# Low parts of the sequence-DFT pieces: GpSimd's subtraction replaced by a negated copy on ScalarE and an accumulating transfer from DRAM

## The chip, the cores and the metric

The kernel runs on one core of one Trainium2 chip. The metric is the device time of one execution in microseconds (us). Beside the timed runs there is one execution recorded by the hardware profiler; its span runs from the first to the last instruction of the program. The engines are named as the profile names them: PE (matrix products; PEld is its weight load), DVE (VectorE), ACT (ScalarE), POOL (GpSimd), and SP, which only issues transfers.

## What is computed

The input is one sequence of 2048 tokens with 640 features, x. Two branches are mixed with a gate per token:

```
g   = sigmoid((x * gate_w).sum(-1))
a   = x @ hid_re.T            b = x @ hid_im.T
A   = seq_re @ a - seq_im @ b                  # real part of a 2-D DFT
s1, s2 = scores of 32 heads against two sets of 16 keys
B   = sum over heads and the best 2 of 256 experts of  gate * gelu(x.u_e) * v_e
out = g * A + (1 - g) * B
```

`seq_re` and `seq_im` are 2048 x 2048, `hid_re` and `hid_im` 640 x 640, all float32. The change concerns `seq_re` and `seq_im` alone.

## The kernel before

**Three products for one.** PE multiplies in fp32r, a float32 with a shorter mantissa. To keep the precision, each float32 matrix is split in two: a high part h, which is the matrix rounded to fp32r, and a low part l = f - h. A product is then three fp32r products, high x high, high x low, low x high (`mm3`, L127 to L129). The helper `split` writes h on ScalarE (L122) and l by a subtraction on the engine that it is given (L123), so all splits in the profile have these two lines, and are told apart by their tiles.

**The sequence product.** The kernel does the sequence part of the DFT first, then the hidden part. The two sequence matrices are cut in 128 pieces of 128 x 512 (256 KB each): two matrices (`w`), four column blocks of 512 (`c`), 16 row tiles (`s`). In one step, `seq_piece(n)`, PE multiplies the five 128-wide slices of the split x tile `X[s]` with piece n and adds to five PSUM banks: 15 matmuls of 128x512. After 16 steps ScalarE copies the five banks to the tile `ST` (L217), DVE multiplies with the gate row (L191), and the result goes to the DRAM scratch `pd` (L198).

**How a piece comes in.** Step n issues the load of piece n+5 on SP's queue into one of five float32 buffers `wf` (L158), then splits piece n+3 into one of the four slots of the tile `WS`: each slot has a high and a low half. So at step n the slot of piece n-1 is written again, which has to wait until PE is through with piece n-1; and what is written is read by PE three steps later. In a step, the first matmul takes h (L127), the second takes l (L128).

**The start.** Piece 0 is split on ScalarE and VectorE. Pieces 1 and 2 are split before the loop, on ScalarE and GpSimd. Between their subtractions and that of piece 3 stand, on GpSimd's queue, the constants of other stages: `kp` (L286), `io` (L288), `identf` (L290), `ident` (L292) and an iota table (L294).

**What shares the steps.** Through the first 16 steps the tiles of x are loaded (`xr`, L235), split, and summed with the gate weights (L255). From step 4 to about step 30, the weights of the score branch `wq` (32 loads of 640 KB, five buffers, `load_wq`, L305) are folded with the keys on PE (L314), transposed and split; a load of `wq` is issued when the matmuls of the load five before it are done. Steps 31 to 70 carry the scores of a token tile (`score_half`) and its top-2 search on DVE. From step 71 on come the split of the hidden matrices into `DD` (`split_dd`, one subtraction on GpSimd in each of ten steps), and then `experts`: one-hot matrices built on DVE (L567 to L569), multiplied on PE (L595), moved out by ScalarE (L576). The last steps prepare sums of the hidden matrices (`ts`), and after step 127 follows the hidden product in 70 steps (L848), which takes its operands from `pd` with the same `split`, the low parts on GpSimd or VectorE, in a ring of the tiles `WP` and `WS`.

**What sets the order.** Each engine runs its own instructions in the order in which the program was written (the table `then` and the credit of `Pump` decide where a background piece is put in); semaphores hold an instruction until its inputs are there. An instruction that waits holds all that stand behind it on its engine. Transfers are issued on SP's queue and on ScalarE's; GpSimd issues none.

Of the kernel before, what the change touches and what calls it, by code (L numbers as in the profile page):

```python
# [8 lines left out]
F32 = mybir.dt.float32  # L9
F32R = mybir.dt.float32r  # L10
F16 = mybir.dt.float16
AF = mybir.ActivationFunctionType
OP = mybir.AluOpType
# [77 lines left out]
def gated_mix_kernel(ctx: ExitStack, tc: tile.TileContext, xT, xn, dreT, dimT, wsre, wsim, wq, kT, uT, vv, gw, out):  # L91
    nc = tc.nc
# [27 lines left out]
    def split(f, h, l, eng):  # L120

        nc.scalar.activation(h, f, AF.Copy)  # L122
        eng.tensor_sub(l, f, h.bitcast(F32))  # L123
# [27 lines left out]
    pieces = [(w, c, s) for w in range(2) for c in range(NC) for s in range(NT)]  # L151
    pf, psp, X, xr = {}, {}, {}, {}
# [7 lines left out]
    WS = big.tile([P, 4, 2, TC], F32R, name="WS", tag="WS")  # L160

    def split_piece(n):
        if n < NPC:
            psp[n] = WS[:, n % 4, 0], WS[:, n % 4, 1]
            split(pf.pop(n), *psp[n], nc.gpsimd)


    then = {}
# [31 lines left out]
    def seq_piece(n):  # L200
        w, c, s = pieces[n]
        if s == 0:
            banks[:] = [bank(d) for d in range(KD)]
        load_piece(n + 5)
        split_piece(n + 3)
        h, l = psp.pop(n)
        if n == 0:
            for a, (x, c) in enumerate(((0, h), (0, l), (1, h))):
                for d in range(KD):
                    nc.tensor.matmul(banks[d], X[0][:, x, d * P:(d + 1) * P], c, start=a == 0, stop=False)  # L210
            return
        for d in range(KD):
            ds = slice(d * P, (d + 1) * P)
            mm3(banks[d], X[s][:, 0, ds], X[s][:, 1, ds], h, l, s == 0, s == NT - 1)
            if s == NT - 1:
                staged[n // NT, d] = f = stage()
                nc.scalar.activation(f, banks[d], AF.Copy)  # L217
            run_bg(0.68)

    for q in range(2 * NC):  # L220
        n = NT * (q + 1)
# [58 lines left out]
    for n in (1, 2):  # L280
        split_x(n)
        split_piece(n)
# [84 lines left out]
    n = bursts[-1]  # L367
# [170 lines left out]
    for p in range(NP):  # L538
        n = N0 + 5 * p
# [467 lines left out]
```

## Time and profile before

| | us |
|---|---|
| median of 3 runs | 777.33 |
| lowest and highest | 776.52, 777.54 |
| the profiled execution | 775.9 |
| its span | 774.1 |

| engine | busy us | share of the span | instructions |
|---|---|---|---|
| PE | 768.1 | 99% | 4628 |
| DVE | 502.2 | 65% | 594 |
| ACT | 283.3 | 37% | 461 |
| POOL | 342.9 | 44% | 233 |

The granted clock of PE was full through the span. The profiled execution took 1.8 us more than its span: what lies around the instructions. It lies 1.4 us under the median of the timed runs. In the profile, a row of the timeline is: start, length, engine, line, operation, tiles (out<-in), shape, and in brackets the idle time before it with what ended it. A row of a window table is: the window, its length, per engine the busy time and the number of instructions, the granted clock, the mean busy share of the core's 16 DMA engines, and what they moved in GB/s. A DMA row gives the number of issues, the size of each, and the time from issue to landing.

### The profile page before, as it was taken

To read this page: it belongs to the slowest core of one execution; us is meant where nothing else is said; L and a number is where in the kernel's file an instruction comes from. 1 tells how busy PE (TensorE), PEld (TensorE's weight loads), DVE (VectorE), ACT (ScalarE), POOL (GpSimd) and SP (SyncE) were. 2 spreads that over 40 slices of the span, in tenths; PEclk is the share of its full clock that TensorE was granted. 3 is DMA by queue.
4 is the path that set the end of the run, shared out by engine and by line. 5 is a ranking of instruction groups with operands and counts; after the bars stand their busy time and mean duration, and the time that the engine had idled before them with its cause. 6 is when DMAs were issued, how large, how long until landed. Compare 5 with 4: busy or idle time off the path is not lost.

```text
span 774.1 us, 11926 instructions
## 1 busy us (share of the span) xinstructions
PE 768.1 (99%) x4628; PEld 622.2 (80%) x4628; DVE 502.2 (65%) x594; ACT 283.3 (37%) x461; POOL 342.9 (44%) x233
## 2 busy tenths in 40 slices
PE   9999999999999999999999999999999999999997
PEld 6777677888888888888888888777788888888886
DVE  6641121276888698689978593687677488628561
ACT  5344323322214432353343453322243453424350
POOL 5523224415144242424332885343346583659270
PEclk9999999999999999999999999999999999999999
DMA  9976985603021530224324454453564694766321
GB/s 349 357 269 192 307 327 191 209 0 116 15 102 35 168 130 2 90 61 136 113 72 151 141 163 112 97 165 92 151 194 160 201 313 162 256 190 203 123 82 68
DMA packets 86792, 121.20 MB, mean 157 GB/s; under 512 B 33104, under 2 KB 40144, under 8 KB 86736
## 3 DMA queue, kind: packets, MB, share of 16 engines
q1 hardware_dynamic: 57344, 100.90, 40.1%
q10 hardware_dynamic: 29392, 19.54, 8.1%
q8 instruction: 36, 0.59, 0.3%
q14 instruction: 20, 0.16, 0.1%
HBM read 98.91 MB, written 19.93 MB: 154 GB/s over the span
## 4 chain that ended last, share of the span: by engine, by line
PE 97%; POOL 1%; DMA 1%; ACT 0%; SPq 0%; issue 0%; ACTq 0%; DVE 0%; DVEq 0%; POOLq 0%
PE b L127 31%; PE b L128 31%; PE b L129 31%; PE b L314 3%; PE b L595 1%; DMA wf<-in_wsre 1%; PE b L326 1%; POOL WS L123 0%; POOL kp L286 0%; ACT L384 0%; SPq L235 0%; SPq L158 0%; POOL identf L290 0%; ACT WS L122 0%; ACT ST L217 0%
## 5 line engine op out<-in xcount | busy, mean ns | idle before, releaser
L123 POOL TENSOR_TENSOR WS<-wf,WS 128x512 fp32r<-128x512 f32 x127 | 190.6, 1506 | 278.0 <-ACT WS L122 256.6
L127 PE MATMUL b<-WS,X 128*128 128x512 f32 x635 | 251.2, 396 | 0.1
L128 PE MATMUL b<-WS,X 128*128 128x512 f32 x635 | 247.9, 390 | 0.2 <-POOL WS L123 0.2
L129 PE MATMUL b<-WS,X 128*128 128x512 f32 x635 | 247.4, 390 | 0.0
L127 PEld LDWEIGHTS b<-WS,X 128*128 128x128 f32 x635 | 119.2, 188 | 33.3 <-issue 7.8
L129 PEld LDWEIGHTS b<-WS,X 128*128 128x128 f32 x635 | 119.2, 188 | 25.2
L128 PEld LDWEIGHTS b<-WS,X 128*128 128x128 f32 x635 | 119.3, 188 | 24.6 <-POOL WS L123 1.1
L122 ACT ACTIVATE WS<-wf 128x512 fp32r<-128x512 f32 x128 | 80.8, 632 | 111.9 <-PE b L129 59.4
L431 DVE TENSOR_REDUCE mm<-sc 128x64 f32<-128x1024 f32 x32 | 39.0, 1219 | 46.2 <-ACT sc L417 45.6
L123 POOL TENSOR_TENSOR xl<-xf,xh 128x640 fp32r<-128x640 f32 x16 | 33.1, 2089 | 70.3 <-ACT xh L122 62.9
L127 PE MATMUL b<-WU,xh 128*128 128x512 f32 x160 | 62.2, 389 | 0.0
L128 PE MATMUL b<-WU,xh 128*128 128x512 f32 x160 | 62.2, 389 | 0.0
L129 PE MATMUL b<-WU,xl 128*128 128x512 f32 x160 | 62.2, 389 | 0.0
L123 POOL TENSOR_TENSOR WS<-ra,WS 128x512 fp32r<-128x512 f32 x32 | 46.2, 1469 | 27.4 <-ACT WS L122 27.4
L417 ACT ACTIVATE sc<-b 128x512 f32<-128x512 f32 x32 | 20.8, 650 | 101.9 <-PE b L129 100.8
L567 DVE TENSOR_TENSOR hot<-rows,wtab 128x1024 f16<-128x1024 f16 x32 | 29.9, 935 | 35.7 <-PE b L595 35.7
L191 DVE SCALAR_TENSOR_TENSOR ST<-ST,grow 128x512 f32<-128x512 f32 x40 | 34.2, 912 | 22.4 <-DMA grow<-gdr 15.5
L433 DVE TENSOR_TENSOR eq<-sc,mm 128x1024 f16<-128x1024 f32 x32 | 45.3, 1416 | 1.1
L741 DVE TENSOR_TENSOR ra<-ra 128x512 f32<-128x512 f32 x40 | 40.7, 1066 | 6.1 <-POOL WS L123 6.1
L329 DVE TENSOR_TENSOR WU<-b,WU 128x512 fp32r<-128x512 f32 (+1 forms) x16 | 7.8, 491 | 56.6 <-ACT WU L328 56.6
L123 POOL TENSOR_TENSOR WP<-ra,WP 128x512 fp32r<-128x512 f32 x18 | 30.4, 1696 | 27.2 <-ACT WP L122 21.5
L497 ACT ACTIVATE rows<-rt 128x384 f16<-128x384 f16 x16 | 31.0, 1968 | 25.3 <-DMA rt<-gs 25.3
(141 smaller groups left out, 1190.6 us busy)
## 6 DMA issues: line engine op xcount, KB each, us to landing
wq<-in_wq SPq DMA_DIRECT2D x32, 640.0 KB, 6.2
ra<-pd SPq DMA_DIRECT2D x70, 256.0 KB, 4.1
wf<-in_wsre SPq DMA_DIRECT2D x64, 256.0 KB, 4.9
wf<-in_wsim SPq DMA_DIRECT2D x64, 256.0 KB, 2.8
pd<-ST ACTq DMA_DIRECT2D x40, 256.0 KB, 3.1
xr<-in_xn SPq DMA_DIRECT2D x16, 320.0 KB, 6.1
xf<-in_xT SPq DMA_DIRECT2D x16, 320.0 KB, 3.2
out_y<-ST ACTq DMA_DIRECT2D x7, 512.0 KB, 3.6
```

The costliest lines, as they stand in the source:

```text
L122: nc.scalar.activation(h, f, AF.Copy)
L123: eng.tensor_sub(l, f, h.bitcast(F32))
L127: nc.tensor.matmul(o, wh, ah, start=first, stop=False, skip_group_check=more)
L128: nc.tensor.matmul(o, wh, al, start=False, stop=False, skip_group_check=more)
L129: nc.tensor.matmul(o, wl, ah, start=False, stop=last, skip_group_check=more)
L191: nc.vector.scalar_tensor_tensor(f, f, -1.0 if w else 1.0, g, op0=OP.mult, op1=OP.mult)
L314: nc.tensor.matmul(ps[32 * j:32 * j + 32, :HALF], kp[:, 8 * G // H, r, :], w[:, j], start=(r == 0), stop=(r == 1))
L431: nc.vector.tensor_reduce(m, sc, op=OP.max, axis=AX.X)
L433: nc.vector.tensor_tensor(eq, sc, m[:, :, None].to_broadcast([P, HH, E]), op=OP.is_equal)
L497: nc.scalar.activation(ROWS[i // 8][:, :, :, i % 8], t, AF.Copy)
L567: nc.vector.tensor_tensor(pt, row(0), wt, op=OP.is_equal)
L741: nc.vector.tensor_add(raw[b, o, k], raw[b, o, k], raw[b, what, k])
```

## The change

Pieces 0, 1 and 2 are split as before. For the other 125 pieces, ScalarE writes h as before, then a second ScalarE instruction reads h and writes -h into the low half of the slot; then GpSimd's queue issues a transfer that reads the same piece from DRAM once more and adds it to what the low half holds, so that it becomes f - h. The subtraction on GpSimd goes. The piece is thus read from DRAM twice, and the low half is ready when the transfer has landed.

```
     def split_piece(n):
         if n < NPC:
-            psp[n] = WS[:, n % 4, 0], WS[:, n % 4, 1]
-            split(pf.pop(n), *psp[n], nc.gpsimd)
+            psp[n] = h, l = WS[:, n % 4, 0], WS[:, n % 4, 1]
+            f = pf.pop(n)
+            if n < 3:
+                split(f, h, l, nc.gpsimd)
+                return
+            w, c, s = pieces[n]
+            nc.scalar.activation(h, f, AF.Copy)
+            nc.scalar.activation(l, h.bitcast(F32), AF.Copy, scale=-1.0)
+            nc.gpsimd.dma_start(l, (wsre, wsim)[w][c, s], accum_op=OP.add)
```

The lines behind it move down by seven; in the changed kernel L170 writes h, L171 writes -h and L172 is the transfer.

How the instructions stand is shown at three places. The first is GpSimd's queue at the start, from the subtractions of pieces 1 and 2 to the last constant and what comes behind it. Before:

```order
L123 TENSOR_TENSOR WS<-wf,WS 128x512 x2
L286 COPY kp<-kt 128x2x16 x2
L288 IOTA io 128x128
L290 TENSOR_SCALAR identf<-io 128x128
L292 CAST ident<-identf 128x128
L294 IOTA wtab_147 128x64
L123 TENSOR_TENSOR WS<-wf,WS 128x512 x28
```

And in the changed kernel:

```order
L123 TENSOR_TENSOR WS<-wf,WS 128x512 x2
L293 COPY kp<-kt 128x2x16 x2
L295 IOTA io 128x128
L297 TENSOR_SCALAR identf<-io 128x128
L299 CAST ident<-identf 128x128
L301 IOTA wtab_147 128x64
L172 DMA WS<-in_wsre 128x512 x28
```

The transfers stand where the subtractions stood: that of piece 3 is still behind the constants.

The second place is ScalarE's queue at the end of the first 16 steps, around the sigmoid of the gate (`gt`) and the copies of the five banks to `ST`. Before:

```order
L384 ACT_TABLE_LOAD
L384 ACTIVATE gt<-zc 128x16
L385 DMA gdr<-gt 128x16x1
L122 ACTIVATE WS<-wf 128x512
L217 ACTIVATE ST<-b_149 128x512
```

And in the changed kernel:

```order
L391 ACT_TABLE_LOAD
L391 ACTIVATE gt<-zc 128x16
L392 DMA gdr<-gt 128x16x1
L170 ACTIVATE WS<-wf 128x512
L171 ACTIVATE WS<-WS 128x512
L224 ACTIVATE ST<-b_149 128x512
```

The write of -h has come between the write of h and the first copy of a bank; so it does at every piece, ahead of whatever ScalarE had next.

The third place is GpSimd's queue in the steps that split the hidden matrices. Before:

```order
L123 TENSOR_TENSOR DD<-draw,DD 128x640
L123 TENSOR_TENSOR WS<-wf,WS 128x512
L123 TENSOR_TENSOR DD<-draw,DD 128x640
L123 TENSOR_TENSOR WS<-wf,WS 128x512
L123 TENSOR_TENSOR DD<-draw,DD 128x640
```

And in the changed kernel:

```order
L123 TENSOR_TENSOR DD<-draw,DD 128x640
L172 DMA WS<-in_wsim 128x512
L123 TENSOR_TENSOR DD<-draw,DD 128x640
L172 DMA WS<-in_wsim 128x512
L123 TENSOR_TENSOR DD<-draw,DD 128x640
```

A transfer stands between two subtractions of `DD` and is issued in turn with them.

## The prediction

> **What bounds the kernel now.** I read the page first: busy shares, chain, and the two groups that the change touches.
>
> ```profile
> PE 768.1 (99%) x4628; PEld 622.2 (80%) x4628; DVE 502.2 (65%) x594; ACT 283.3 (37%) x461; POOL 342.9 (44%) x233
> ...
> PE 97%; POOL 1%; DMA 1%; ACT 0%; SPq 0%; issue 0%; ACTq 0%; DVE 0%; DVEq 0%; POOLq 0%
> ...
> L123 POOL TENSOR_TENSOR WS<-wf,WS 128x512 fp32r<-128x512 f32 x127 | 190.6, 1506 | 278.0 <-ACT WS L122 256.6
> ...
> L122 ACT ACTIVATE WS<-wf 128x512 fp32r<-128x512 f32 x128 | 80.8, 632 | 111.9 <-PE b L129 59.4
> ```
>
> PE is busy 99% of the span and carries 97% of the chain. The subtractions cost 190.6 us on GpSimd, but GpSimd is 44% busy. Next, the waits of PE: who could give it time back?
>
> ```profile
> PE b L274 <- DVE warm L271: 1.2, 1, 1.2
> PE b L210 <- ACT WS L122: 0.5, 1, 0.5
> PE b L128 <- POOL WS L123: 0.2, 1, 0.2
> ```
>
> That is the whole list. PE waits 0.2 us for GpSimd in all, at piece 3. So a lighter GpSimd gives PE at most 0.2 us, and no gain can be seen. A difference of 0.2% (1.6 us) is about what a measurement of this kernel tells from none. What is left to ask is what the new way of making l costs where l is due. I go through the four places where its time is short, then through the load on the DMA engines.
>
> **Part 1: piece 3.** The timelines of ScalarE, GpSimd and PE at the start:
>
> ```profile
> 10.48 0.63 ACT L122 ACTIVATE WS<-wf 128x512 fp32r<-128x512 f32 x1 [0.82 <-DMA wf<-in_wsre]
> ...
> 14.24 0.26 POOL L294 IOTA wtab<- 128x64 f16 x1
> ...
> 16.16 0.50 PE L128 MATMUL b<-WS,X 128*128 128x512 f32 x1 [0.21 <-POOL WS L123]
> ```
>
> The last constant ends at 14.50 and the transfer can't be issued before. -h is ready by then: h ends at 11.11, and -h takes another 0.63 us (the 632 ns of L122). PE took l at 16.16. If L is the time from issue to landing, the change costs L - 1.66 us here. The trace has no transfer issued by GpSimd and none that accumulates. The nearest rows are plain 256 KB transfers: the loads of the first 19.4 us, the five stores that came from another queue (ScalarE's) in 58 to 135 us, and the loads of 471 to 617 us, with their shortest.
>
> ```profile
> wf<-in_wsre SPq DMA_DIRECT2D x10, 256.0 KB, 5.0
> ...
> pd<-ST ACTq DMA_DIRECT2D x5, 256.0 KB, 8.0
> ...
> wf<-in_wsim SPq DMA_DIRECT2D x33, 256.0 KB, 2.7
> ...
> DMA to landing us min/median/max: 2.5/2.7/6.0
> ```
>
> L lies between 2.5 and 8.0; I take 5.0, the row of the same place and time. Piece 3 then comes 3.3 us late (0.8 to 6.3). Piece 4 is due one step later and queued one transfer behind; PE, late by piece 3, meets it.
>
> **Part 2: the table load at 67 us.** ScalarE's timeline, and PE's:
>
> ```profile
> 69.30 0.63 ACT L122 ACTIVATE WS<-wf 128x512 fp32r<-128x512 f32 x1 [0.55 <-ACT gt L384]
> 69.84 2.53 ACT L217 ACTIVATE ST<-b 128x512 f32<-128x512 f32 x5
> ...
> 70.00 0.39 PE L129 MATMUL b<-WS,X 128*128 128x512 f32 x1
> 70.47 0.50 PE L127 MATMUL b<-WS,X 128*128 128x512 f32 x1
> ```
>
> Matmuls follow each other every 0.23 us; here 0.47, because the first bank is copied late. -h comes between, so PE waits 0.7 us more (0.63 and the pass from one instruction to the next). Elsewhere ScalarE, 37% busy, takes 125 x 0.63 = 79 us more beside PE's work.
>
> **Part 3: the steps that split `DD`.** Here l was closest: piece 85.
>
> ```profile
> 455.44 0.74 ACT L122 ACTIVATE DD<-draw 128x640 fp32r<-128x640 f32 x1 [5.29 <-DVE hot L568]
> 456.09 0.62 ACT L122 ACTIVATE WS<-wf 128x512 fp32r<-128x512 f32 x1
> ...
> 456.26 1.72 POOL L123 TENSOR_TENSOR DD<-draw,DD 128x640 fp32r<-128x640 f32 x1 [3.28 <-ACT DD L122]
> 457.94 1.75 POOL L123 TENSOR_TENSOR WS<-wf,WS 128x512 fp32r<-128x512 f32 x1
> ...
> 461.25 0.39 PE L128 MATMUL b<-WS,X 128*128 128x512 f32 x1
> ```
>
> The -h of piece 84 puts ScalarE 0.7 us back, so `DD` goes to GpSimd at about 456.9 and its subtraction ends at 458.6; behind it, in order, stands the transfer. At L = 5.0 it lands at 463.6, 2.4 us late (0 at 2.5, 5.4 at 8.0). The next pieces follow with the delay gained.
>
> **Part 4: the dense steps.** ScalarE writes h of a piece, PE takes its l three steps of 3.40 us later:
>
> ```profile
> 586.56 0.63 ACT L122 ACTIVATE WS<-wf 128x512 fp32r<-128x512 f32 x1 [1.34 <-POOL ts L123]
> 589.96 0.63 ACT L122 ACTIVATE WS<-wf 128x512 fp32r<-128x512 f32 x1 [2.77 <-PE b L129]
> ...
> 596.73 0.39 PE L128 MATMUL b<-WS,X 128*128 128x512 f32 x1
> ```
>
> From the end of h at 587.19 to 596.73 there are 9.5 us; less 0.7 for -h, L may be 8.8. At 5.0 it costs nothing, and even at 8.0. The cover is the four slots of `WS`; beyond 8.8 each four steps would last as long as a step and the landing, so a step grows by a third of the excess. Two windows hold such steps, 28 writes of h in 94 us:
>
> ```profile
> 417.00:471.00 54.00, 10.35 (x16) 1.00 0.50 159
> 567.00:607.00 40.00, 7.00 (x12) 1.00 0.55 172
> ```
>
> In the steps between, PE has expert matmuls to do as well, and the steps in the score branch are twice as long: more room than here.
>
> **Part 5: the DMA engines up to 135 us.** While x, `wq` and the pieces come in together, the engines have little room. The windows, asked for the tile `wf` alone, give ScalarE's writes of h with the share of the DMA engines (over all transfers):
>
> ```profile
> 0.00:19.40 19.40, 4.38 (x7) 1.00 0.93 349
> 19.40:38.70 19.30, 3.17 (x5) 1.00 0.96 357
> 38.70:58.00 19.30, 2.81 (x5) 1.00 0.74 270
> 58.00:77.40 19.40, 2.91 (x5) 1.00 0.65 191
> 77.40:135.00 57.60, 7.53 (x12) 1.00 0.81 274
> 573.00:617.00 44.00, 6.92 (x11) 1.00 0.57 178
> ```
>
> The counts to 135 us make 34; one lies across a border, three pieces keep the subtraction: 30 transfers are added. Used are 18.0 + 18.5 + 14.3 + 12.6 + 46.7 = 110.1 us of 135, free 24.9. In the second window 357 GB/s at 0.96 are 372 GB/s for all engines, so 0.262 MB passes in 0.70 us. An accumulating transfer fetches two operands, the piece and what the low half holds. No row shows its cost. From below it is one pass, 0.70; from above I put three (2.11: two fetches and the write back one after the other). I take two, 1.41, because two operands are fetched where a load fetches one. Then 30 x 1.41 = 42.3 us are asked of 24.9: 17.4 too many.
>
> The Trainium skill, Collectives: The Full Stack, section The bandwidth ceiling: the fold count and why AG ≠ RS ≠ AR, says of a reducing transfer that the addition itself costs no cycles, but that its two source reads share one read ring, and so halve the rate. By it the price is the two passes. No run so far shows it.
>
> How much of that PE feels depends on the slack of `wq`, which PE itself eats:
>
> ```profile
> L314 PE MATMUL b<-wq,kp x144: 432/432/458, 79.5 to 128.3; 128*32 128x320 f32 x144
> L305 SPq DMA_DIRECT2D wq<-in_wq x13: 327/328/1162, 80.3 to 118.0; - x13
> ...
> DMA to landing us min/median/max: 3.9/7.0/9.3
> ```
>
> The last load is issued at 118.0, lands 7.0 later and is used at about 128: 3 us of slack. PE comes 17.4 - 3 = 14.4 us late by then. The 3.3 us of part 1 lie within it: while PE waits there, the engines work off the same queue. Later, in 573 to 617 us, 11 more of 1.41 (15.5 us) fit in the free 18.9 us.
>
> **The sum.** 14.4 + 0.7 + 2.4 = 17.5 us on the profiled execution's 775.9: 793.4. The timed median is 1.4 above that execution, so 794.8; I say 794.
>
> **The rivals.** *One pass (chance 0.25):* the addition is free beside a load's time. 30 x 0.70 = 21.1 us fit in the 24.9; what stays is 3.3 + 0.7 + 2.4 = 6.4, so 783.7. For it: the second operand lies in SBUF, not DRAM. Against: it too is fetched by the same 16 engines.
>
> *Three passes, or too long a landing (0.21):* at 2.11 us, 63.3 asked, less 24.9 and 3, is 35.4; with 3.1, 815.8. Or L passes 8.8, and each of the 28 steps of part 4 grows by a third of the excess: at 12 us by 1.07, with the other terms 777.3 + 17.5 + 30 = 825. The 8.0 row, at a share of 0.81, speaks for it; the 2.7 row in just these steps against.
>
> *Not slower (0.06):* one place decides, piece 3. If the transfer lands within 3.2 us of issue, PE loses under 1.6 there, and with short landings nothing at piece 85; one pass must hold as well. The time would be 777 to 779. For it: loads land in 2.5 to 2.7 us in quiet windows. Against: at 14.5 us the share is 0.93.
>
> The Trainium skill, DMA: Bandwidth & Descriptors, section Anatomy of one DMA — SWDGE (gpsimd) path, puts a transfer from GpSimd at 2.0 us plus its bytes at 436 GB/s. By that estimate 256 KB land in 2.6 us and piece 3 loses 0.9, this rival's case; the loaded rows here are twice that.
>
> That the change does not do what it says, so that GpSimd writes descriptors as long as it subtracted, changes nothing: it has room, and the time would be that of the other cases.
>
> **The numbers.** The forecast has 0.48. Its own range, L from 2.5 to 8.0 at piece 85 (0 to 5.4 us) and a slack of 0 to 8 us, is 777.3 + 10.1 to 777.3 + 23.5: 787 to 801. Down to 780 it takes in the one-pass case, up to 822 three passes and the shorter overruns; left out are the case of no change and the far overruns, some 0.14. Faster 0.01, since PE's waits hold 0.2 us; same 0.05; slower 0.94.
>
> **What would show it.** Right: PE waits for the transfer into `WS` at L128 of piece 3 for 3 us or more; shares of the DMA engines near 1.0 up to 135 us, and waits of PE at L314 for `wq` or in `mm3` for x; a shift of 10 us or more by 150 us, hardly any between 150 and 440. Wrong: shares that grow by half of what I say (one pass), a step of over 3.40 us at 580 us (landing over 8.8), or no wait at piece 3.

## The result and the profile after

The changed kernel takes 800.67 us (median of 798.50, 800.67 and 807.24) against 777.33 before: a ratio of 1.0322, 95% interval 1.0227 to 1.0416. The profiled execution took 798.5 us against 775.9, and its span is 796.7 against 774.1: PE loses 22.6 us. The three runs lie further apart than those of before, and in the order of their granted clock (0.996, 0.991, 0.987).

First the page of the changed kernel: busy shares, the queues of the DMA engines (packets, MB, share of 16 engines' span), and the two new groups.

```profile
PE 773.4 (97%) x4628; PEld 622.0 (78%) x4628; DVE 447.1 (56%) x594; ACT 357.7 (45%) x586; POOL 260.7 (33%) x233
...
q1 hardware_dynamic: 57344, 100.90, 38.4%
q0 software_dynamic: 18000, 32.78, 26.3%
...
L172 POOL DMA_DIRECT2D WS<-in_wsre x61 | 54.0, 924 | 217.2 <-ACT WS L171 192.4
...
L171 ACT ACTIVATE WS<-WS 128x512 fp32r<-128x512 f32 x125 | 79.2, 633 | 4.0
```

GpSimd's load fell from 342.9 to 260.7 us and VectorE's from 502.2 to 447.1, and neither bought anything. ScalarE's rose by 74.4. The new queue q0 took 26.3% of 796.7 us for 125 transfers: 1.68 us of all 16 engines for each. A plain transfer of the same 0.262 MB on q1 took 0.262 / 100.90 of 38.4%: 0.80 us. The ratio is 2.1, close to two passes. That is what the rule of two source reads in the prediction (the Trainium skill, Collectives: The Full Stack, section The bandwidth ceiling: the fold count and why AG ≠ RS ≠ AR) makes of it. The page states it of the reduction step of a collective; the trace agrees in size. Experiment 4 shows how much of it hangs on the addition.

PE's list of waits (us in total, times, longest), which held 1.9 us before:

```profile
PE b L128 <- DMA WS<-in_wsre: 6.1, 1, 6.1
PE b L128 <- DMA WS<-in_wsim: 5.6, 4, 2.5
PE b L321 <- DMA wq<-in_wq: 2.8, 2, 1.6
PE b L127 <- ACT ST L224: 1.4, 3, 0.7
PE b L281 <- DVE warm L278: 1.2, 1, 1.2
PE b L333 <- ACT wp L327: 1.1, 1, 1.1
PE b L127 <- ACT sc L424: 0.5, 1, 0.5
PE b L217 <- ACT WS L122: 0.4, 1, 0.4
```

Where the time went is read from the start of the last matmul of a piece in both traces:

| piece | before | after | late by |
|---|---|---|---|
| 2 | 15.34 | 15.61 | 0.3 |
| 3 | 19.24 | 26.92 | 7.7 |
| 32 | 146.24 | 159.24 | 13.0 |
| 73 | 423.40 | 438.04 | 14.6 |
| 85 | 464.20 | 484.39 | 20.2 |
| 96 | 505.76 | 528.21 | 22.5 |
| 127 | 620.08 | 642.66 | 22.6 |

There are two places: the first 150 us (13.0 us, more than half of it at piece 3) and the steps that split `DD` (7.8 us from 74 to 96). The hidden product adds nothing. Of the 7.8 us, 1.2 arise at piece 74, 1.6 at 81, 2.8 at 85, 1.7 at 86 and 87, and 0.5 at 96. PE's waits at pieces 74, 81 and 85:

```profile
439.56 0.50 PE L128 MATMUL b<-WS,X 128*128 128x512 f32 x1 [0.91 <-DMA WS<-in_wsim]
...
464.92 0.50 PE L128 MATMUL b<-WS,X 128*128 128x512 f32 x1 [1.26 <-DMA WS<-in_wsim]
...
481.31 0.50 PE L128 MATMUL b<-WS,X 128*128 128x512 f32 x1 [2.46 <-DMA WS<-in_wsim]
```

At piece 3, GpSimd's timeline, then PE's:

```profile
14.79 2.83 POOL L172 DMA_DIRECT2D WS<-in_wsre  x3
22.52 0.89 POOL L172 DMA_DIRECT2D WS<-in_wsre  x1 [4.90 <-issue]
```

```profile
22.31 0.80 PE L128 MATMUL b<-WS,X 128*128 128x512 f32 x1 [6.08 <-DMA WS<-in_wsre]
22.90 0.63 PE L129 MATMUL b<-WS,X 128*128 128x512 f32 x1
23.33 0.63 PE L127 MATMUL b<-WS,X 128*128 128x512 f32 x1
```

The transfer is issued at 14.79, as soon as the constants are through, and PE takes l at 22.31, where it took it at 16.16 before: 6.15 us late. Behind the wait the matmuls are 0.63 long and 0.43 apart, where they were 0.39 and 0.23: the granted clock is at half until 25.5, which costs the other 1.25 us.

The landing times of the transfers, from GpSimd's issue, in four stretches: 0 to 30, 135 to 430, 430 to 500 (the steps that split `DD`) and 500 to 643 us:

```profile
DMA to landing us min/median/max: 4.4/7.5/10.7
...
DMA to landing us min/median/max: 4.0/4.8/8.8
...
DMA to landing us min/median/max: 4.1/6.9/8.9
...
DMA to landing us min/median/max: 4.2/5.1/7.5
```

In the third stretch the transfers of pieces 74, 81 and 85 took 8.1, 8.9 and 4.2 us.

The windows of the prediction's part 5, moved with PE (tile `wf` alone; the last two columns are the share of the DMA engines and GB/s; a share above 1 means that the times of packets on one engine overlap):

```profile
0.00:22.50 22.50, 0.69 (x1) 4.39 (x7) 2.62 (x2) 0.92 0.94 330
22.50:38.70 16.20, 0.00 (x0) 1.90 (x3) 0.00 (x0) 0.90 1.04 301
38.70:58.00 19.30, 0.00 (x0) 2.49 (x4) 0.00 (x0) 1.00 1.05 341
58.00:77.40 19.40, 0.00 (x0) 2.99 (x5) 0.00 (x0) 1.00 1.05 324
77.40:148.00 70.60, 0.00 (x0) 9.01 (x15) 0.00 (x0) 1.00 0.99 291
585.00:640.00 55.00, 0.00 (x0) 8.21 (x13) 0.00 (x0) 1.00 0.96 236
```

Used are 21.2 + 16.8 + 20.3 + 20.4 + 69.9 = 148.5 of 148 us, where 110.1 were used to the same place before (135). The engines are full; the 30 transfers added 38.4 us, 1.28 each.

### The profile page after: what moved, and what is told of

Its sections match the earlier page's. It is cut to its first block, busy times and chain, and to the rows that moved or that the text cites. A ratio compares the mean times of both kernels' runs of the same rounds, so it can differ in the third digit from the quotient of the medians.

```text
span 796.7 us, 12119 instructions
## 1 busy us (share of the span) xinstructions
PE 773.4 (97%) x4628; PEld 622.0 (78%) x4628; DVE 447.1 (56%) x594; ACT 357.7 (45%) x586; POOL 260.7 (33%) x233
## 3 DMA queue, kind: packets, MB, share of 16 engines
q1 hardware_dynamic: 57344, 100.90, 38.4%
q0 software_dynamic: 18000, 32.78, 26.3%
## 4 chain that ended last, share of the span: by engine, by line
PE 73%; issue 9%; DMA 8%; POOL 4%; DVE 2%; SPq 1%; ACT 1%; ACTq 0%; POOLq 0%; DVEq 0%
PE b L127 24%; PE b L128 23%; PE b L129 23%; DMA wq<-in_wq 4%; POOL DD L123 2%; PE b L321 2%; POOL WS L172 1%; PE b L602 1%; DMA WS<-in_wsre 1%; DMA WS<-in_wsim 1%; DMA wf<-in_wsim 1%; DMA rt<-gs 1%; DMA wf<-in_wsre 1%; DMA draw<-in_dimT 0%; POOL xl L123 0%
## 5 line engine op out<-in xcount | busy, mean ns | idle before, releaser
L172 POOL DMA_DIRECT2D WS<-in_wsre x61 | 54.0, 924 | 217.2 <-ACT WS L171 192.4
L170 ACT ACTIVATE WS<-wf 128x512 fp32r<-128x512 f32 x125 | 78.8, 630 | 100.9 <-PE b L129 57.6
L172 POOL DMA_DIRECT2D WS<-in_wsim x64 | 56.6, 894 | 161.3 <-ACT WS L171 146.5
L171 ACT ACTIVATE WS<-WS 128x512 fp32r<-128x512 f32 x125 | 79.2, 633 | 4.0
L424 ACT ACTIVATE sc<-b 128x512 f32<-128x512 f32 x32 | 21.5, 671 | 82.4 <-PE b L129 81.0
L574 DVE TENSOR_TENSOR hot<-rows,wtab 128x1024 f16<-128x1024 f16 x32 | 22.0, 689 | 59.8 <-PE b L602 59.8
L198 DVE SCALAR_TENSOR_TENSOR ST<-ST,grow 128x512 f32<-128x512 f32 x40 | 27.1, 738 | 37.2 <-ACT WS L171 18.6
L122 ACT ACTIVATE WS<-ra 128x512 fp32r<-128x512 f32 x46 | 28.3, 631 | 31.9 <-PE b L129 10.2
```

Of the source, the lines that this page charges most:

```text
L171: nc.scalar.activation(l, h.bitcast(F32), AF.Copy, scale=-1.0)
L172: nc.gpsimd.dma_start(l, (wsre, wsim)[w][c, s], accum_op=OP.add)
L198: nc.vector.scalar_tensor_tensor(f, f, -1.0 if w else 1.0, g, op0=OP.mult, op1=OP.mult)
```

## The experiments

**The theory.** Two causes, apart from each other. Up to 150 us the DMA engines have no room for a second fetch (the budget), and PE's delay is the excess, wherever it shows first. In the steps that split `DD`, instructions that wait in order stand ahead of the transfer. **The rivals:** the delay at piece 3 is a landing time by itself, and what comes later are its followers; or each transfer costs about the same, wherever it is. A wait of PE is also suspected to cost more than itself, by the clock.

The delay of PE in each profiled execution, against before, in us, by the pieces at which it arose. The sum is the difference of the spans:

| kernel | to 3 | 4 to 32 | 33 to 73 | 74 to 96 | later | sum |
|---|---|---|---|---|---|---|
| changed kernel | 7.7 | 5.3 | 1.6 | 7.8 | 0.2 | 22.6 |
| 1: start at piece 6 | 0.1 | 9.6 | 0.2 | 7.0 | 0.1 | 16.9 |
| 2: to piece 32 only | 7.8 | 9.2 | 0.0 | 0.0 | 0.1 | 17.1 |
| 3: from piece 33 only | 0.4 | 0.0 | 0.6 | 8.4 | 0.2 | 9.6 |
| 4: no addition | 7.7 | 2.5 | 0.0 | 2.4 | 0.1 | 12.6 |
| 5: -h alone | 0.5 | 0.7 | 0.4 | 4.2 | 0.0 | 5.8 |
| 6: GpSimd held | 8.9 | 0.0 | 0.0 | 0.0 | 0.0 | 8.9 |
| 7: ballast | 0.4 | 15.2 | 2.9 | 7.0 | 4.3 | 29.8 |
| 8: ring | 8.2 | 7.4 | 0.9 | 7.8 | 0.4 | 24.6 |
| 9: pieces 73 to 96 only | 0.0 | 0.0 | 0.0 | 6.1 | 0.2 | 6.3 |
| 10: 33 to 72, 97 to 127 | 0.9 | 0.0 | 0.4 | 0.6 | 0.2 | 2.1 |

**1. Pieces 3 to 5 keep the subtraction.**

```diff
-            if n < 3:
+            if n < 6:
```

> Pieces 3, 4 and 5 keep the subtraction on GpSimd; transfers from piece 6 on. Budget theory (the DMA engines are full up to 150 us and that alone sets the delay; the wait at piece 3 lies within it): three transfers fewer take off 3 x 1.35 = 4.0 us, PE is 9 us late by step 32 instead of 13, and the time is about 4 us under the changed kernel's, some 796 us. Rival (separate waits: piece 3 is one loss with the clock drop behind it, the waits for wq another): 7.4 us go, PE is 5.6 us late by step 32, some 792 us; the granted clock is 1.00 throughout.

795.51 us (before 776.66; ratio 1.0229, 1.0197 to 1.0261). The wait at piece 3 is gone, and yet 9.6 of the 13.0 us stay: three transfers less are 3.8 us of engine time less, 9.2. If piece 3's 7.4 us had been its own, 5.6 would have been left. PE's waits in this kernel:

```profile
PE b L128 <- DMA WS<-in_wsim: 4.1, 2, 3.3
PE b L128 <- DMA WS<-in_wsre: 3.5, 2, 1.7
PE b L127 <- ACT ST L224: 1.5, 3, 0.7
PE b L321 <- DMA wq<-in_wq: 1.4, 1, 1.4
```

The wait moved to other pieces and to `wq`. For the first stretch this agrees with the budget. It doesn't exclude the rival by itself, since the delay by piece 32 differs between executions: with the same early transfers it is 13.0 us in the changed kernel, 17.0 in experiment 2 and 15.6 in experiment 8. Experiment 7 settles it.

**2 and 3. The early pieces alone, the late ones alone.**

```diff
-            if n < 3:
+            if n < 3 or n > 32:      # experiment 2
+            if n < 33:               # experiment 3
```

> Transfers for pieces 3 to 32 alone, the subtraction for all others. Both theories of the start: PE is 13 us late by step 32, as in the changed kernel, and stays so: 777.3 + 13 = 790 us. If the later waits are caused by the early ones (work pushed back), more would remain, up to 800.

> The subtraction for pieces 0 to 32, transfers from piece 33 on. The later waits are their own: 22.6 - 13.0 = 9.6 us, 787 us, with PE not late at step 32 and the waits at pieces 74, 81, 85 to 87 and 96 in place. Rival (the later waits come from the backlog of the start): under 2 us, 779 us.

792.09 us (1.0188, 1.0146 to 1.0231) and 786.76 us (1.0131, 1.0093 to 1.0169). Alone they cost 15.4 and 10.1 us, together 25.5, against 23.3 of the change: two causes that don't need each other. In experiment 2 PE was 17.0 us late by piece 32, where the expectation had 13. That the late half loses 8.4 us at pieces 74 to 96 with nothing ahead of it speaks against followers.

**4. No addition.** The transfer writes f to the low half instead of adding it (the low parts are then f, and the addition is left out).

```diff
-            nc.gpsimd.dma_start(l, (wsre, wsim)[w][c, s], accum_op=OP.add)
+            nc.gpsimd.dma_start(l, (wsre, wsim)[w][c, s])
```

> The transfer from GpSimd writes the piece into the low half without adding (the low part is then f and not f - h; the product has f in the place of l); -h is still written before it. Budget theory with two fetches for an accumulating transfer: one fetch makes 0.7 us of the 1.35, 30 x 0.7 = 21 us fit in the free 24.9, waits for wq go, the landing takes about 5 us, piece 3 is 3 to 4 us late: about 785 us. Rival (the second fetch is free; what costs is the issue by GpSimd and the wait for landing): as the changed kernel, 797 us or more, share of the software queue unchanged at 26%.

789.37 us (1.0155, 1.0128 to 1.0181): between theory and rival. The queue's row on the page:

```profile
q0 software_dynamic: 18000, 32.78, 16.5%
```

16.5% of the span of 786.7 us is 1.04 us for each, so the addition costs 0.64 of the 1.68: against the same transfer without it, an accumulating one takes 1.6 times as long. The rest of the ratio of 2.1 comes with GpSimd's queue, where even a plain transfer takes 1.04 against 0.80. All waits for `wq` are gone, the later half of the first 13 us falls from 5.3 to 2.5 and the `DD` steps from 7.8 to 2.4. Piece 3 is 7.7 late as before, though its transfer lands in 6.5 us instead of 7.5 and PE waits 1.0 less:

```profile
21.40 0.79 PE L128 MATMUL b<-WS,X 128*128 128x512 f32 x1 [5.08 <-DMA WS<-in_wsre]
```

That the delay is the same is chance: the granted clock is at half for 6.8 us in both kernels, but here 5.3 of them (to 26.7) lie behind the wait, where PE multiplies, instead of 3.2. Of the 7.5 us, 1.0 comes with the addition. Why the other 6.5 are more than the 5.0 of SP's loads stays open. My expectation had a landing in about 5 us; that part fell.

**5. -h alone.** ScalarE writes -h, then GpSimd subtracts as before (no transfer; it overwrites -h).

```diff
-            nc.gpsimd.dma_start(l, (wsre, wsim)[w][c, s], accum_op=OP.add)
+            nc.gpsimd.tensor_sub(l, f, h.bitcast(F32))
```

> ScalarE writes h and -h as in the changed kernel, but GpSimd then writes the low half by the subtraction of before (the -h is overwritten); no transfers are added. Measures ScalarE's part alone. Theory: 0.6 us at the table load, 0.8 us each where the first score bank and a bank of ST are copied late (pieces 50 and 64), and 1 to 3 us at piece 85, where ScalarE is put back and the subtraction had 1.6 us of slack: 780 to 782 us. Rival (ScalarE, 37% busy, costs PE nothing): 777 to 778 us.

779.53 us against 776.1 (1.0046, 1.0030 to 1.0061): 3.4 us in the median. The profiled execution, the longest of the four, loses 5.8: 3.7 at piece 85, where PE waits 1.8 us and the clock falls to half for 3.4 us, 0.7 at piece 16 (the table load), and 0.4 to 0.5 each at the start and at pieces 64 and 96. At piece 85 -h is not the whole cause. `DD`'s h comes 2.1 us later than before while PE itself is 1.6 late, so ScalarE takes only some 0.5 of the 1.6 us of slack. The wait comes from the subtraction of `DD` ahead of the piece, which took 1.72 us before:

```profile
458.40 5.10 POOL L123 TENSOR_TENSOR DD<-draw,DD 128x640 fp32r<-128x640 f32 x1 [4.22 <-ACT DD L122]
```

Meanwhile VectorE runs its comparisons; the last section comes back to this.

**6. A wait without DMA.** The kernel before, with eight small GpSimd instructions ahead of piece 3's subtraction.

```diff
     nc.gpsimd.iota(wtab, ...)
+    hold = p1.tile([P, P], F32)
+    for _ in range(8):
+        nc.gpsimd.tensor_scalar(hold, io, 0.0, None, op0=OP.is_equal)
```

> The kernel before with eight small instructions more on GpSimd's queue ahead of the subtraction of piece 3, which then ends at about 22.4 us instead of 16.1; no transfers are added and DMA is as before. Measures what a wait of PE of some 6 us at that place costs by itself. Theory (the wait also brings a drop of the granted clock to a half for 6.8 us, in which PE loses 1.5 us): the clock drops, PE is 7.4 to 7.8 us late from piece 3 on, 785 us. Rival (the drop has another cause): no drop, 6.2 us late, 783.5 us.

784.41 us (1.0103, 1.0087 to 1.0118). PE's waits, and windows around the wait (the column behind the five engines is the granted clock):

```profile
PE b L128 <- POOL WS L123: 6.9, 1, 6.9
```

```profile
0.00:17.60 17.60, 14.16 (x54) 9.49 (x54) 10.02 (x17) 9.70 (x15) 8.88 (x17) 1.00 0.91 335
17.60:27.80 10.20, 5.20 (x12) 4.13 (x13) 2.58 (x6) 0.74 (x1) 8.32 (x9) 0.50 0.57 216
```

A wait of 6.9 us costs 8.9, and the clock is at half for 10.2 us though GpSimd issues no transfer: the wait alone brings the clock down. Nothing is lost or won later.

**7. Ballast.** The kernel before keeps its subtraction, and GpSimd issues the same 125 accumulating transfers into a tile that nothing reads.

```diff
+    JK = big.tile([P, 2, TC], F32, name="JK", tag="JK")      # zeroed once
...
             split(pf.pop(n), *psp[n], nc.gpsimd)
+            if n >= 3:
+                w, c, s = pieces[n]
+                nc.gpsimd.dma_start(JK[:, n % 2], (wsre, wsim)[w][c, s], accum_op=OP.add)
```

> The kernel before, with the subtraction, plus the same accumulating transfers from piece 3 on into a tile that nobody reads (two slots in turn), so that their load on the DMA engines is there and nobody waits for their landing. ScalarE writes no -h. Budget theory: the DMA engines are full up to 150 us as in the changed kernel and PE is 11 to 13 us late by step 32 through late wq and x, with no wait at piece 3; hardly anything later: 789 us. Rival (what costs is the wait for the low half; the load alone only shows in the waits for wq): 4 to 6 us late, 782 us.

805.50 us (1.0376, 1.0354 to 1.0398). Nobody waits for these transfers, there is no wait at piece 3, and PE is 15.6 us late by piece 32, all the same. The first two of its waits:

```profile
PE b L319 <- DMA wq<-in_wq: 7.5, 3, 3.3
PE b L128 <- POOL WS L123: 2.8, 3, 2.3
```

All of the waits for `wq`, but only 0.5 us of those for the subtraction, lie before 165 us. This shows the budget by itself, with more than the 11 to 13 us that were expected. Behind 150 us, where the run loses another 14 us, it says little: GpSimd subtracts and issues there, and the tile has only two halves, so that a transfer that waits for the one before it holds the subtractions behind it.

**8. A longer ring.** The memory in which GpSimd's transfers are described, from 1024 to 2048 bytes.

```diff
-    nc = bacc.Bacc("TRN2", ..., dynamic_dma_scratch_size=1024)
+    nc = bacc.Bacc("TRN2", ..., dynamic_dma_scratch_size=2048)
```

> The changed kernel with twice the scratch for the descriptors of GpSimd's transfers (2048 instead of 1024 bytes a partition). In the changed kernel GpSimd issued three transfers from 14.8 to 17.6 us and the fourth only at 22.5 us, when the first had landed. If the scratch holds three accumulating transfers, the fourth now follows the third at about 18 us; if GpSimd waits for something else, it stays at 22.5 us. The time stays within the spread of the changed kernel in both cases, since piece 6 is due at 38 us.

One run, 800.49 us. GpSimd's timeline:

```profile
14.82 2.82 POOL L172 DMA_DIRECT2D WS<-in_wsre  x3
18.14 0.86 POOL L172 DMA_DIRECT2D WS<-in_wsre  x1 [0.51 <-ACT WS L171]
```

The fourth transfer, held to 22.52 in the changed kernel, now follows at 18.14 as soon as its -h is there. So it was the ring that held it. The time lies within the spread of the changed kernel, and one run can't tell more; PE is 8.2 us late at piece 3, where the ring plays no part.

**9 and 10. The late pieces cut in two:** the steps that split `DD`, and all others.

```diff
-            if n < 3:
+            if not 72 < n < 97:              # experiment 9
+            if n < 33 or 72 < n < 97:        # experiment 10
```

> Only pieces 73 to 96 (the steps that split DD, and those behind them) take the new way, the other 104 the subtraction. Theory: nearly all of what the late pieces cost comes from the order of the queues there: DD's instructions and ScalarE's extra 0.63 us stand ahead of a transfer that has to land. PE loses 7 to 8.5 us, about 784 to 785 beside 776.5. Rival: the late cost belongs to the transfers as such, the same for each (9.6 us over the 95 of the run of pieces 33 and on, 0.1 each): 24 of them cost 2.4 us, 779.

> The rest of the late pieces: 33 to 72 and 97 to 127, the quiet and the dense steps, where a landing of up to 8.8 us has room. Theory: PE loses only what lies at 50 and 51 and about 96 (0.6 to 1.5 us): 777 to 778 beside 776.5. Rival, the same cost for each transfer: 71 of them cost 7.2 us, 783.7.

783.33 us (before 776.51; 1.0098, 1.0083 to 1.0113) and 777.73 us (1.0018, 1.0009 to 1.0027). 24 transfers cost 6.8 us, the other 71 together 1.2: the cost is one of place. Why it is so dear there, in experiment 9: the landing times of what is issued in 430 to 462 us (`rt` are transposing transfers on SP's queue), then before's row for `rt`:

```profile
WS<-in_wsim POOLq DMA_DIRECT2D x8, 256.0 KB, 7.0
...
rt<-rp SPq DMA_TRANSPOSE x6, 7.6
```

```profile
rt<-rp SPq DMA_TRANSPOSE x8, 3.8
```

The DMA engines' share, 440 to 465.4 us, in experiment 9 and before:

```profile
440.00:465.40 25.40, 22.42 (x98) 17.92 (x96) 12.91 (x17) 17.05 (x26) 13.37 (x12) 1.00 0.97 231
```

```profile
440.00:465.40 25.40, 25.40 (x114) 21.04 (x113) 21.10 (x17) 16.17 (x22) 18.89 (x12) 1.00 0.59 183
```

And ScalarE, GpSimd and PE at piece 85:

```profile
451.34 7.23 ACTq L205 DMA_DIRECT2D pd<-ST  x5
458.62 0.74 ACT L122 ACTIVATE DD<-draw 128x640 fp32r<-128x640 f32 x1 [5.34 <-DMA rt<-rp]
```

```profile
459.45 1.91 POOL L123 TENSOR_TENSOR DD<-draw,DD 128x640 fp32r<-128x640 f32 x1 [7.30 <-ACT DD L122]
461.30 0.89 POOL L172 DMA_DIRECT2D WS<-in_wsim  x1
```

```profile
465.42 0.51 PE L128 MATMUL b<-WS,X 128*128 128x512 f32 x1 [2.03 <-DMA WS<-in_wsim]
```

The engines are at 0.97 instead of 0.59, and this shows in two ways.

At pieces 74 and 81 the landing alone is too long. GpSimd issues the transfer right behind its -h, with nothing ahead of it, and it takes 7.6 and 8.8 us; PE is 0.7 and 1.3 us later for it. In experiment 4, where the same transfers took 7.0 and 6.5 us, PE lost nothing at either.

At piece 85 it is a chain through the queues. VectorE is through with its products for `pd` at 452.57 (449.86 before). But of ScalarE's five stores of them the last four go out at 455.62, 456.19, 456.88 and 458.24, each right behind the landing of an earlier transfer whose semaphore it uses again: at 455.54 (`rt`), 456.11 (`wf`), 456.81 (the first store) and 458.17 (`rt`). So ScalarE's queue is held to 458.57 instead of 455.40, `DD`'s h starts at 458.62 instead of 455.44, GpSimd's subtraction of `DD` stands behind it, and behind that the transfer, issued at 461.30. The landing itself, 4.1 us, is short. PE, 2.0 us late by pieces 74 and 81, waits 2.03 us, and the granted clock is 0.56 over the next 3.4 us; piece 85 costs 3.9 in all. In experiment 10, with no transfers there, `DD`'s h starts at 455.66. My expectation had put nearly all of the cost down to the order of the queues; that holds for piece 85, but not for 74 and 81.

## Why the prediction was right or wrong

**The bound: right.** PE waited 0.2 us for GpSimd before, so 82 us less work on GpSimd gained nothing. The sign, and the range of 780 to 822, held.

**Part 5, the budget: right in mechanism and nearly in size.** I said two passes of 0.70 us, 1.41 together, and 14.4 us by the last `wq`. The windows give 1.28, the queue row over the whole run 1.68 against 0.80 for a load, and PE is 13.0 - 0.6 (part 2) = 12.4 us late by piece 32. That the size came so near is in part luck, as experiments 2 and 8 gave 17.0 and 15.6 with the same early transfers. That piece 3's loss lies within it is what experiment 7 shows, where the delay by piece 32 is 15.6 without a wait at piece 3; experiment 1, with 9.6, agrees. That the 573 to 617 us stretch has room held as well: the share is 0.96 there, and nothing is lost.

**Part 1, piece 3: mis-sized.** I took L = 5.0, from the loads of the same place and time; the transfer took 7.5, near the upper bound of 8.0. The wait is 6.15 instead of 3.3 us, and 1.25 more by the clock, on which the prediction had no step. Neither enters the sum, for the reason just given.

**Part 2, the table load: right.** 0.7 said, 0.6 measured at piece 16.

**Part 3, the `DD` steps: the step that failed.** 2.4 us said, 7.8 measured (5.9 at pieces 74 to 85 in experiment 9). The prediction let one piece stand for the stretch: "Here l was closest: piece 85", and "The next pieces follow with the delay gained." (In before l was ready 1.6 us ahead of PE at piece 85, but 1.3 at 86 and 1.0 at 87.) At piece 85 PE did wait 2.46 us in the changed kernel, but that is luck, since two things were off. "The -h of piece 84 puts ScalarE 0.7 us back" moved before's timeline by -h's own time and left all that ScalarE waits for where it was; in experiment 9 it came 3.2 us later, since the stores ahead of it wait for landings. Against that, PE itself came 2.0 us later, and L was 4.1 instead of 5.0. The rest of the 7.8 arose at pieces that the prediction gave no cost: 74 and 81, where L was 8.1 and 8.9 instead of 5.0, then 86, 87 and 96. In before l was ready 6.3 and 8.2 us ahead of PE at 74 and 81, which did not look close. I had looked for the DMA engines' limit in the first 135 us alone; the 0.50 of 417 to 471 us is a mean over bursts.

**Part 4, the dense steps: right in one of its two windows.** In the second (567 to 607 us) nothing is lost: landings stay under the 8.8 us of room, at most 7.5 from 500 to 643 us, and experiment 10's 71 transfers cost 1.2 us. The first (417 to 471 us) is the stretch of part 3, and there the 8.8 us did not cover piece 81.

**Not on the list:** 1.6 us at pieces 50 and 64, where ScalarE copies late (`L424`, `L224`); in experiment 10, 0.4 are left of it.

**The sum:** 17.5 said, 22.6 measured on the profiled execution: 2.0 less in part 5, 5.4 more in part 3, 1.7 that were not seen or are small. **The rivals:** one pass is refuted by the queue rows, and even where there was one fetch (experiment 4) the time was 789.4, not 783.7, because all of piece 3's delay stayed, 2.5 us at pieces 4 to 32, and 2.4 in the `DD` steps. Three passes and a landing of piece 3 within 3.2 us did not occur. A landing over 8.8 us did, at piece 81 (8.9), but no step of the window behind 567 us grew by it. The estimate of 2.6 us for a landing, from the Trainium skill, DMA: Bandwidth & Descriptors (Anatomy of one DMA — SWDGE (gpsimd) path), is below every accumulating transfer of the changed kernel: the shortest took 4.0.

## What to carry to other kernels

Before work is moved from an engine to a transfer, ask which stretch of the kernel has room on the DMA engines, and count an accumulating transfer twice; where there is none, PE is late by the excess, whichever wait shows it first. A mean share over 50 us is not room: at 0.50 before, the stretch of 417 to 471 us still had landings of 8 to 9 us with the new transfers in it. In a stretch with little slack, don't shift a queue by the new instruction's length alone: look up what stands ahead in that queue and whether it waits for a transfer too. Used only where both have room (experiment 10), the change costs 0.2%, but gains nothing either, as GpSimd was not what PE waited for.

## What the runs showed of the hardware

**A wait costs PE its clock.** After the waits of 6.1 us (changed kernel) and 6.9 us (experiment 6) the granted clock is at half for 6.8 and 10.2 us, part of it still within the wait; after 2.03 us (experiment 9) it is 0.56 for 3.4 us. Not each wait does it: after 2.46 us in the changed kernel it stayed at 1.00.

```profile
476.00:481.30 5.30, 2.85 (x13) 2.04 (x11) 0.00 (x0) 5.24 (x7) 4.16 (x5) 1.00 0.87 227
481.30:486.00 4.70, 4.54 (x19) 3.45 (x20) 0.00 (x0) 4.60 (x7) 3.31 (x4) 1.00 0.68 125
```

The Trainium skill, TensorE: Matmul & The Clock Gate, section Part 1: The HAM clock gate (the "warmup" mystery), speaks of half rate after an idle window of some 3.4 us, counted in windows that run freely. Lengths of 3.4, 6.8 and 10.2 us agree with such windows; but a wait of 2.03 us was enough here, short of that window. Whether the lower clock of the run at 807 us (0.987) is such a wait more is open.

**Two engines were at odds before.** VectorE's one-hot comparisons, in the groups of before and of the changed kernel:

```profile
L567 DVE TENSOR_TENSOR hot<-rows,wtab 128x1024 f16<-128x1024 f16 x32 | 29.9, 935 | 35.7 <-PE b L595 35.7
```

```profile
L574 DVE TENSOR_TENSOR hot<-rows,wtab 128x1024 f16<-128x1024 f16 x32 | 22.0, 689 | 59.8 <-PE b L602 59.8
```

The same instruction takes 689 instead of 935 ns once GpSimd no longer subtracts the pieces; in experiment 5, where it does, 801, and there one subtraction on GpSimd took 5.10 instead of 1.72 us while VectorE ran six comparisons and products at 0.68 to 0.69 each. The Trainium skill, SBUF — State Buffer, section SBUF: two separate sides, says that an instruction of VectorE with two inputs in SBUF and one of GpSimd that reads there exclude each other; these numbers agree. VectorE's busy time fell by 55 us in all, and PE did not wait for VectorE.
